# A fused attention and gated-MLP block on one Trainium2 core: the head (loads, modulation, first block of q, k and v) is rebuilt

## The chip, the core and the metric

The kernel runs on one NeuronCore of a Trainium2 chip. The core has five engines with instruction streams of their own: TensorE (PE in the profile; its weight loads are shown apart as PEld), VectorE (DVE), ScalarE (ACT), GpSimd (POOL) and SyncE (SP, which only issues DMAs). They share an on-chip memory of 128 partitions. Matmul results go to PSUM, which has 8 banks of 512 float32 per partition. Engines wait for one another, and for DMAs, by semaphores, and each works strictly in the order of its own stream. The metric is the device time of one execution in microseconds (us); lower is better.

## The reference

x is [2048, 448] in bf16. A conditioning vector c gives six rows of 448 numbers, `silu(c) @ w_mod`: shift, scale and gate for each of two blocks.

```python
mod = (_silu(c) @ w_mod).reshape(c.shape[0], 6, 1, -1)
sa, ca, ga, sb, cb, gb = ...
h = _layernorm(x, axis=-1) * (1 + ca) + sa
x = x + ga * _A_ref(h, A_wqkv, A_wo)
h = _layernorm(x, axis=-1) * (1 + cb) + sb
x = x + gb * _B_ref(h, B_w_in, B_w_sp, B_b_sp, B_w_out)
```

`_A_ref` is attention with 16 heads of 28 dims, causal with a window of 256 keys. `_B_ref` is a gated MLP: `z = gelu(h @ w_in)` with 1792 columns, the second half layer-normed and mixed over the 2048 rows by a 2048 x 2048 matrix, the product of the halves times `w_out`.

## The kernel before, in words

The 2048 rows are 16 tiles of 128 rows (t or j), in four blocks of 512 (tb). The 448 columns of x are four chunks of 128, 128, 128 and 64 (kc or ch).

**The head.** x tiles 0 to 3 (`t_x0`, L415), the first two sixths of w_mod (`t_wmA`, L419: shift and scale of block A) and the q and k columns of wqkv (`t_wq`, L420) are loaded from the SP and ACT queues by `load3` (L406), which puts chunks 0 and 1 into one DMA on ACT and chunks 2 and 3 on SP. The loads of wv, x tiles 4 to 7 and the rest of w_mod (`t_wmB`) wait until `t_wmA` has landed (L422 to L428). c is turned into a column by four small matmuls (L507) and goes through silu. `mod_cols` (L520) multiplies w_mod by it: shift and scale come out as columns (`modT`), one matmul per chunk pair. This is done for block A once w_mod's first part is there (`t_mA`) and for block B later (`t_mB`). The two gates ga and gb are needed along the free axis in all partitions, so the silu column is repeated 128 times (`sc_rep`) and multiplied by w_mod (L574), and VectorE copies the result out (`gg_sb`, L577). GpSimd multiplies wo and w_out by the gates (L580, L929). `warm` (L556) puts matmuls on the identity into gaps of TensorE.

**Block 0** is normed by `stats` (L588: VectorE statistics, GpSimd's reciprocal root) and `norm` (L601), turned on TensorE (L660), scaled and shifted on the way out of PSUM into `hT` (L672/L674, 512 columns), and multiplied by `WQK` (the q and k weights copied to heads of 32, L583) into eight groups of 512 columns (L689) and by wv into V (L742). Block 1 goes the same way. Blocks 2 and 3 are turned by DMA (`turn`, L463) and scaled in place (L653/L655). The q of a block is spread into a block-diagonal buffer `QBD` by four DMAs (L720), whose zeros ACT writes (L516).

**Attention.** For each tile j and each half of the heads: scores (L818 for j 0 and 1, L844 and L853 after), exp on ACT (L805), masks on VectorE (L860, L880), the product with V (L887), the division (L901, L903), a DMA transpose, the product with wo (L912), a second layer norm and another DMA transpose. Then the MLP: the halves of `h @ w_in` (L997, L1018), the mixing matmuls (L1041), add on VectorE (L1045), product on GpSimd (L1048), the product with w_out (L1058), the last add (L1068) and the store (L1073).

**What sets the order.** Every operation is added to a list and gets a number. `ORDER` (L19) is a table that names each operation that is emitted, in order, with its engine (p, a, v, g, s) and the PSUM banks or buffers that it takes. Where an operation may run on two or three engines (`either`, `free`), the table chooses. `Sched.waits` (L208) puts the semaphore waits in. Warm-ups that are not in the table are not emitted. The durations in the code only weigh choices; nothing on the chip waits for them.

Of the kernel before, what the change touches and what calls it, by code (L numbers as in the profile page):

```python
# [4 lines left out]
ACT = mybir.ActivationFunctionType  # L5
# [14 lines left out]
2.a 21.v 30.g 1.s 22.v 23.v 24.v 33.g 34.g 0.a 4.s 31.g 3.a 28.g 25.v 5.s 32.g 6.a 26.v 35.g 50.v 51.p.0 7.s 40.a 8.s 52.p.1 36.g 107.v 53.p.2 109.v  # L20
37.g 108.v 115.v 41.p.0 29.g 38.g 110.v 54.p.3 117.v 39.g 42.a 111.g 43.a 116.v 112.g 118.v 44.a 55.p.4 119.g 113.v.0 45.a 56.p.5 120.g 114.v.1
123.p.1 9.s 121.v.2 49.p.0 122.v.3 10.s 105.a 11.s 106.a 127.p.2 12.s 103.v 104.g 124.p 88.v 128.p 89.v 90.v 13.s 91.v 57.p.3 125.a 129.v 58.p.4 130.a
126.v 131.p.5 59.p.0 132.p 133.p 134.p 136.p.3 135.a 138.p.4 46.a 48.v 146.p.1 147.a 164.v 162.v 168.v 163.v 166.v 167.v 165.v 169.v 170.g 171.g 139.a
142.p.0 143.a 150.s 172.g 151.s 149.s 176.g 174.g 178.g 173.g.0 179.g.1 140.p.2 141.a 137.a 148.s 14.s 16.s 15.s 18.s 17.s 154.p.1 152.p.0 323.p.0
155.v 144.p.1 153.v 145.v 95.p.0 324.a.0 177.v.2 96.v 325.v 175.v.3 327.v 156.p.1 329.p.0 157.a 330.a.1 47.a 97.p.0 98.v 180.p.1 326.p.0 348.p.0 328.p
183.p.0 377.p.0 181.v 182.v 92.p.1 349.a.2 350.a 355.p.0 356.a.3 357.a 331.v 184.v 333.v 185.v 214.v 351.v 94.v 93.v 218.v 158.p.0 332.p 192.p.1 334.p
159.v 186.p.0 375.p.0 193.a 187.a 376.a.4.0 219.v 216.v 27.v 217.v 220.v 215.v 221.v 190.p.1 188.p.0 358.v 335.v 353.v 336.v.0 272.v 191.v 274.v 360.v
273.v 379.v 380.v 270.v 352.p.0 354.p 222.g 223.g 224.g 226.g 228.g 225.g.0 227.g.1 230.g 231.g.2 229.g.3 189.a 378.a 337.s 383.p.0 359.p 160.p.0
385.p.0 198.p.1 361.p 384.a.5.1 161.a 386.a 404.p.0 199.v 362.v 363.v.1 200.p.0 204.p.1 381.p.0 406.p.0 405.a.6.2 407.a 268.v 201.v 409.v 205.v 271.v
388.v 269.v 275.v 387.v 408.v 232.s 235.s 234.s 233.s 196.s 194.s 195.s 197.s 412.p.0 382.p 212.p.0 414.p.0 202.p.1 213.v 413.a.0.3 203.a 433.p.0  # L30
389.p 390.p 210.p.1 208.p.0 434.a.1.4 415.a 209.a 441.p.0 442.a.2.0 417.v 391.v 392.v.2 416.v 410.p.0 411.p 418.p 419.p 437.v 211.v 238.v 435.p.0
# [233 lines left out]
def bass_adaLN_cond__sliding_block__mixer_gmlp__prompt_kernel(  # L265
# [15 lines left out]
    NT = S // 128  # L281
# [859 lines left out]
```

## Time and profile before

| | us |
|---|---|
| median of 3 runs | 281.21 (279.92 to 281.25) |
| profiled execution, first to last instruction (its span; the page gives no other time for it) | 281.0 |
| PE busy | 269.3 |
| DVE busy | 164.3 |
| ACT busy | 128.5 |
| POOL busy | 126.1 |
| start of the first q/k matmul | 15.34 |
| start of the first exp | 23.61 |

The page gives the busy time of each engine, the span in 40 slices, the DMA queues, the chain of work that ended last, and the costliest groups of instructions. A timeline row reads: start, duration, engine, line, operation, tile written <- tile read, count; in brackets the idle time before it and what ended that. A row of the stretches reads: from:to, length, then busy us (and instructions) of PE, PEld, DVE, ACT and POOL, the granted TensorE clock, the share of the DMA engines, and GB/s.

### The profile page before, as it was taken

How to read it: one execution, taken by the hardware profiler on the slowest of the kernel's cores; microseconds unless marked ns; L12 is line 12 of the kernel's file. 1: busy time of each engine (PE TensorE's matmuls, PEld its weight loads, DVE VectorE, ACT ScalarE, POOL GpSimd, SP SyncE). 2: the span in 40 equal slices, each digit the busy share in tenths (PEclk: the TensorE clock that was granted, in tenths of full speed). 3: DMA queues.
4: the chain of work that ended last, by engine and by line, in shares of the span. 5: the costliest groups of instructions: out<-in, count | busy, mean ns of one | idle time of the engine just before them, and what ended most of it. 6: DMA issues, size and time to landing. Idle time of an engine off the chain costs nothing.

```text
span 281.0 us, 7380 instructions
## 1 busy us (share of the span) xinstructions
PE 269.3 (96%) x3198; PEld 142.3 (51%) x3222; DVE 164.3 (58%) x355; ACT 128.5 (46%) x151; POOL 126.1 (45%) x200
## 2 busy tenths in 40 slices
PE   6799999799999999999999999999999999999995
PEld 2445556456657777544444444444444444444452
DVE  6347999599899999968898600000243003124443
ACT  4548899789999999866666700000000000000000
POOL 8231177921027989947769503001477101436110
PEclk9789999999999999999999999999999999999999
DMA  6775735343315485693699989910000000000032
GB/s 199 188 261 157 267 58 98 84 55 72 72 23 75 63 96 80 162 103 79 125 181 186 168 181 201 163 36 0 0 2 0 0 0 2 16 16 16 19 98 98
DMA packets 65347, 26.01 MB, mean 93 GB/s; under 512 B 56418, under 2 KB 64227, under 8 KB 65315
## 3 DMA queue, kind: packets, MB, share of 16 engines
q1 hardware_dynamic: 64496, 24.39, 43.6%
q10 hardware_dynamic: 818, 1.15, 1.5%
q8 instruction: 25, 0.41, 0.6%
q14 instruction: 8, 0.06, 0.1%
HBM read 9.01 MB, written 1.84 MB: 39 GB/s over the span
## 4 chain that ended last, share of the span: by engine, by line
PE 80%; POOL 5%; DVE 4%; ACT 4%; issue 3%; DMA 3%; ACTq 0%; POOLq 0%
PE ps L1041 34%; PE ps L997 8%; PE ps L1058 8%; PE ps L1018 8%; PE ps L689 6%; PE ps L887 4%; ACT PW L805 3%; PE ps L912 3%; DMA wmod<-in_w_mod_dram 3%; PE ps L844 2%; PE ps L742 2%; PE ps L853 1%; POOL xn L610 1%; PE ps L729 1%; POOL wo_g L580 1%
## 5 line engine op out<-in xcount | busy, mean ns | idle before, releaser
L805 ACT ACTIVATE PW<-ps 128x2048 bf16<-128x2048 f32 (+1 forms) x56 | 67.8, 1240 | 4.3 <-PE ps L844 2.6
L1048 POOL TENSOR_TENSOR z1T<-tmpg,z1T 128x512 bf16<-128x512 bf16 x28 | 31.7, 1152 | 77.9 <-DVE tmpg L1045 77.9
L1045 DVE TENSOR_TENSOR tmpg<-ps,bsp_bc 128x512 bf16<-128x512 f32 x28 | 19.0, 689 | 79.2 <-PE ps L1041 70.3
L1041 PE MATMUL ps<-wspB,z 128*128 128x512 bf16 x219 | 49.2, 379 | 0.3
L1041 PE MATMUL ps<-wspA,z 128*128 128x512 bf16 x219 | 48.9, 379 | 0.4 <-issue 0.2
L860 DVE TENSOR_TENSOR PT<-PW,mask 128x1024 bf16<-128x1024 bf16 x56 | 39.2, 729 | 0.3 <-ACT PW L805 0.2
L1041 PEld LDWEIGHTS ps<-wspA,z 128*128 128x128 bf16 x224 | 21.8, 98 | 26.6 <-issue 0.4
L1041 PEld LDWEIGHTS ps<-wspB,z 128*128 128x128 bf16 x224 | 21.9, 98 | 26.3
L596 POOL TENSOR_SCALAR ve_all<-mv_all 128x1 f32<-128x1 f32 (+2 forms) x37 | 11.3, 312 | 46.7 <-DVE mv_all L594 45.9
L689 PE MATMUL ps<-hT,WQK 128*128 128x512 bf16 x98 | 25.5, 388 | 2.4 <-POOL hT L655 1.4
L597 POOL TENSOR_TENSOR rs_all<-ve_all,neghalf 128x1 f32<-128x1 f32 (+2 forms) x37 | 25.3, 694 | 1.1
L887 PE MATMUL ps<-Vaug,PT 128*128 128x32 bf16 x496 | 24.4, 177 | 0.5 <-DVE PT L860 0.5
L887 PEld LDWEIGHTS ps<-Vaug,PT 128*128 128x128 bf16 x496 | 21.8, 96 | 4.4 <-DVE o_sb L903 0.9
L997 PE MATMUL ps<-w_in,hT 64*128 64x448 bf16 x224 | 22.7, 349 | 0.2 <-ACT PW L805 0.2
L1018 PE MATMUL ps<-hT,w_in 64*128 64x512 bf16 x196 | 22.3, 376 | 0.0
L1058 PE MATMUL ps<-w_out_g,z1T 128*128 128x448 bf16 x112 | 21.8, 353 | 0.0
L887 PE MATMUL ps<-Vaug,PW 128*128 128x32 bf16 x224 | 20.2, 176 | 0.0
L591 DVE BATCH_NORM_STATS2 st_all<-x_sb 128x6 f32<-128x448 bf16 x32 | 19.2, 610 | 0.4 <-DMA x_sb<-in_A_x_dram 0.4
L610 POOL TENSOR_SCALAR xn<-x_sb,rs_all,ve_all 128x448 bf16<-128x448 bf16 x22 | 18.9, 863 | 0.3
L887 PEld LDWEIGHTS ps<-Vaug,PW 128*128 128x128 bf16 x224 | 17.6, 96 | 1.9
L591 DVE BATCH_NORM_STATS2 st_all<-z 128x6 f32<-128x448 bf16 x32 | 18.1, 602 | 0.2 <-ACT z L1004 0.2
L1004 ACT ACTIVATE z<-ps 128x896 bf16<-128x896 f32 x16 | 14.1, 915 | 8.3 <-PE ps L997 8.2
(100 smaller groups left out, 333.1 us busy)
## 6 DMA issues: line engine op xcount, KB each, us to landing
out_dram<-fin SPq DMA_DIRECT2D x16, 112.0 KB, 1.7
x_sb<-in_A_x_dram SPq DMA_DIRECT2D x3, 448.0 KB, 4.9
wmod<-in_w_mod_dram SPq DMA_DIRECT2D x1, 1344.0 KB, 8.6
w_in<-in_B_w_in_dram SPq DMA_DIRECT2D x1, 1344.0 KB, 8.9
QBD<-qT SPq DMA_DIRECT2D x16, 64.0 KB, 2.0
w_out_g<-in_B_w_out_dram SPq DMA_DIRECT2D x1, 784.0 KB, 5.3
bsp_bc<-in_B_b_sp_dram SPq DMA_DIRECT2D x1, 512.0 KB, 6.8
wmod<-in_w_mod_dram SPq DMA_DIRECT2D x2, 224.0 KB, 6.1
```

The source lines that it names most:

```text
L591: st = [dve(0.62 if True else 0, lambda e, t=t, ci=ci, s=s: e.bn_stats(st_all[:, slot, t, ci, :], s()), deps(t), prio) for ci, s in enumer ...
L597: rs = pool(0.53 + 0.15 * len(tiles), lambda e: e.tensor_tensor(rs_all[:, slot, a:b], ve_all[:, slot, a:b], neghalf[:, 0:b - a], ALU.pow), ...
L610: "pool": (0.9, lambda e: e.tensor_scalar(to[:, h.slot[0], 0:D], x_sb[:, t, :], z, ve, ALU.mult, ALU.add))}, [nm], prio, [h])
L689: mms = [lambda e, h=h, g=g, kc=kc, tb=tb: e.matmul(ps[:, h.slot[0], :], lhsT=WQK[:, kc, 4 * g:4 * g + 4, :].rearrange("p a b -> p (a b)") ...
L805: ex = act(xdur, lambda e, out_ap=out_ap, in_ap=in_ap: e.activation(out_ap(), in_ap(), ACT.Exp, scale=SCALE), [s], v - 8.0 + u, takes, tab ...
L860: return dve(0.70, lambda e: e.tensor_tensor(cols(hp.slot[0] * 2048 + 1024 * k, [[256, 4], [128, 2], [1, 128]]), cols(at_w() + 128 + 192 * ...
L887: fns.append(lambda e, hp=hp, hO=hO, hi=hi, bi=bi, kb=kb, hd=hd, nb=nb, a=at[hi][bi], p_of=p_of: e.matmul(ps[:, hO.slot[0], 32 * hd:32 * h ...
L997: return lambda e, kc, p0, start, stop: e.matmul(ps[:, hs[t % 2].slot[hf], 0:D], lhsT=hT[p0:p0 + 64, kc, t * 128:(t + 1) * 128], rhs=w_in[ ...
L1018: return lambda e, kc, p0, start, stop: e.matmul(ps[:, hs[b // 2].slot[b % 2], :], lhsT=w_in[p0:p0 + 64, kc, ft * 128:(ft + 1) * 128], rhs ...
L1041: m = pe(16 * MMS, [lambda e, h=h, si=si, ft=ft, tb=tb: e.matmul(ps[:, h.slot[0], :], lhsT=z2[:, si, ft * 128:(ft + 1) * 128], rhs=(wspA i ...
L1048: u = pool(1.16, lambda e, ht=ht, ft=ft, tb=tb: e.tensor_tensor(z1T[tb][:, ft, :], tmpg[:, ht.slot[0], :], z1T[tb][:, ft, :], ALU.mult), [ ...
L1058: return [lambda e, ft=ft: e.matmul(ps[:, h.slot[0], 0:D], lhsT=z1T[t // 4][:, ft, (t % 4) * 128:(t % 4 + 1) * 128], rhs=w_out_g[:, ft, :] ...
```

## The change

- **Loads.** w_mod (first 960 columns now) and the q/k weights come as four row chunks each, alternating between the SP and ACT queues, each with a semaphore of its own. wv, x tiles 4 to 7 and the rest of w_mod no longer wait for `t_wmA`. x tiles 8 to 15 are now issued ahead of the q spread of block 0; in the old order they were issued behind it. wo and w_in still come behind it, with w_in behind block 2's four DMA transposes.
- **Modulation of block A.** A row of ones is put into chunk 3 of w_mod and a 1 into the silu column, so that the matmul also adds the 1 of 1 + scale. The products of each chunk go to columns of their own (8 matmuls per chunk, as each chunk lands), and one VectorE reduction adds them.
- **Gates, and shift and scale of block B.** 16 matmuls in column strips of 32 (`t_rows`) give the four rows; one copy takes them out, two DMAs write them to a DRAM buffer `modrow`, and three DMAs read them back: each gate spread over 128 partitions, shift and scale as columns, four bytes at a time.
- **Block 0** is worked off in two halves of 256 columns. In the first half every q/k group is four matmuls of their own that the order table may mix. Attention of tiles 0 and 1 depends on the first half only.
- **Other.** Three of the four QBD zero fills go from ACT to GpSimd, the first of them ahead of the identity. Warm-ups are one matmul each and use bank 5; 11 are in the table (9 pairs before). The output of tile 1 is made in two halves of 224 columns.
- **The order table** is new from end to end. In it tile 15 is the last output; before it was tile 1. Two of the four scale-and-shift steps of block 2, which ran on GpSimd, are on VectorE and ACT, as are the other two.

```diff
-    t_wmA = load3("d_wmA", wmod, w_mod, slice(0, 2 * D), -98.95, 7.75, 4.5, 6.7)
-    t_wq = load3("d_wq", wq_st, A_wqkv, slice(0, 2 * D), -98.9, 9.6, 8.4, 9.4)
-
-    t_wv = load2("d_wv", "sp", 0.35, wv, ALL, A_wqkv, slice(2 * D, 3 * D), [t_wmA], -95.5)
+    t_wmA = [chunk("d_wmA", ("sp", "act", "sp", "act")[kc], wmod, w_mod, kc, slice(0, 2 * D + 64), -98.95 + 0.001 * kc, LAND_M[kc], 0.23) for kc in range(DC)]
+    t_wq = [chunk("d_wq", ("sp", "act", "sp", "act")[kc], wq_st, A_wqkv, kc, slice(0, 2 * D), -98.9 + 0.001 * kc, LAND_Q[kc], 0.23) for kc in range(DC)]
+
+    t_wv = load2("d_wv", "sp", 0.35, wv, ALL, A_wqkv, slice(2 * D, 3 * D), (), -95.5)
...
-    t_x.append(load_x(1, [t_wmA], -95.0))
-    t_wmB = load2("d_wmB", "sp", 1.4, wmod, slice(2 * D, 6 * D), w_mod, slice(2 * D, 6 * D), [t_wmA], -94.0)
+    t_x.append(load_x(1, (), -95.0))
...
+    t_wmB = load2("d_wmB", "sp", 1.4, wmod, slice(2 * D + 64, 6 * D), w_mod, slice(2 * D + 64, 6 * D), (), -94.0)
...
+    t_qz = [[add({"act": (1.05, lambda e, b=b, q=q: e.activation(QBD[:, b, q].rearrange("p h t -> p (h t)").bitcast(F32), zero[:, 0:1].broadcast_to([128, 1024]), ACT.Copy)),
+                  "pool": (1.3, lambda e, b=b, q=q: e.memset(QBD[:, b, q].rearrange("p h t -> p (h t)").bitcast(F32), 0.0))},
...
+        t_mA.append(pe(0.37, [lambda e, v=v, ch=ch, kc=kc, n=n: e.matmul(
+            ps[:, hA.slot[0], 8 * kc + n:8 * kc + n + 1], lhsT=wmod[:, kc, v * D + ch * 128:v * D + ch * 128 + 128], rhs=sc_sb[:, kc:kc + 1],
+            start=True, stop=True)
...
+    t_modA = [dve(0.16, lambda e: e.tensor_reduce(modT[:, 0:8], ps[:, hA.slot[0], 0:32].rearrange("p (k n) -> p n k", k=4), mybir.AxisListType.X, ALU.add), [t_mA], -59.0)]
...
+    t_rows = pe(0.8, [lambda e, v=v, i=i, kc=kc: e.matmul(
+        ps[32 * i:32 * i + 32, hR.slot[0], 0:D], lhsT=sc_rep[:, kc, :], rhs=wmod[:, kc, v * D:(v + 1) * D],
+        start=(kc == 0), stop=(kc == DC - 1), tile_position=(0, 32 * i)) for kc in range(DC) for i, v in enumerate((2, 5, 3, 4))],
+        [t_wmA, t_wmB, t_screp, t_p2], -15.0, [hR], "cols32")
...
+    t_rowd = [load("d_mr0", "sp", 0.01, lambda e: e.dma_start(modrow[:, 0:D], rows4[0:128:32, :]), [t_rowc], -14.95),
+              load("d_mr1", "sp", 0.01, lambda e: e.dma_start(modrow[2:4, D:DP], rows4[64:128:32, D - 64:D]), [t_rowc], -14.9)]
+    t_gg = [load("d_mg%d" % gi, "sp", 0.1, lambda e, gi=gi: e.dma_start(gg_sb[:, gi, :], modrow[gi:gi + 1, 0:D].broadcast_to([128, D])), [t_rowd[0]], -14.8) for gi in range(2)]
+    t_mc = load("d_mc", "sp", 0.05, lambda e: e.dma_start(modT[:, 8:16], modrow[2:4, :].rearrange("v (c p) -> p (v c)", p=128), allow_slow_non_contiguous=True), [t_rowd], -14.7)
...
+    for half in range(2):
...
+        for g in (0, 4, 1, 5, 2, 6, 3, 7):
+            h = Hold(bA)
+            parts = [lambda e, h=h, g=g, kc=kc, c0=c0: e.matmul(
+                ps[:, h.slot[0], 0:256], lhsT=WQK[:, kc, 4 * g:4 * g + 4, :].rearrange("p a b -> p (a b)"), rhs=hT[:, kc, c0:c0 + 256],
+                start=(kc == 0), stop=(kc == DC - 1)) for kc in range(DC)]
+            m = None
+            if half == 0:
+                for kc in range(DC):
+                    m = pe(0.109, parts[kc], [evs[kc], t_wqk[kc], m], v + 1 + kc * 0.1 + 0.01 * g, [] if kc else [h])
+            else:
+                m = pe(0.436, parts, [evs, t_wqk], v + 1 + 0.1 * g, [h])
...
+            if t == SPLIT:
+                for c0 in (0, 224):
```

The start of each engine's new order, from the table. SP: x tiles 0 and 1; w_mod chunks 0 and 2; q/k chunks 0 and 2; wv; x 4 to 7; rest of w_mod; x 8 to 11; x 12 to 15; write of the rows; two of four q spreads; gate ga; two q spreads; wo; block 2's transposes; w_in. ACT: x 2 and 3; c; w_mod chunks 1 and 3; table load and silu; q/k chunk 1; silu of c; one zero fill; q/k chunk 3; the copies of q/k chunks 1 and 3 with the first scale-and-shift between them. PE: six warm-ups, c, two warm-ups, w_mod chunks 0 to 2, a warm-up, the turn of tile 0, chunk 3, the turn of tile 1, two warm-ups, the turns of tiles 2 and 3, then q and k of the first half. VectorE before those: the copy of q/k chunk 0, the norm of tile 2, the reduction, the norm of tile 3, three scale-and-shifts.

More of the change, by code (lines that the diff above doesn't have):

```diff
@@ L557, in warm @@
+    hA.until += t_modA
+    def warm(n, dur, times, cols):
         for _ in range(n):
[L558 removed]
+            hW = Hold(bH)
             hW.until.append(pe(dur, [lambda e, hW=hW: e.matmul(
[L560 to L565 removed]
```

380 lines of the change are left out of this document (207 added, 173 removed).

## The prediction

> **What bounds the kernel now.** I read the stretches first (busy time of each engine from:to), then the page's DMA issues, then the timeline of each engine over the head.
>
> ```profile
> span 281.0 us, 7380 instructions
> 0.00:15.34 15.34, 10.83 (x70) 5.53 (x72) 7.64 (x26) 7.17 (x10) 7.93 (x21) 0.82 0.73 210
> 15.34:16.60 1.26, 1.26 (x4) 0.45 (x3) 1.04 (x3) 0.00 (x0) 0.00 (x0) 0.50 1.01 393
> 16.60:22.30 5.70, 5.70 (x28) 2.69 (x27) 2.20 (x8) 4.20 (x7) 3.51 (x8) 0.98 0.41 147
> 22.30:60.00 37.70, 34.83 (x705) 20.30 (x712) 33.18 (x72) 33.05 (x35) 19.78 (x27) 1.00 0.52 126
> 60.00:140.00 80.00, 79.16 (x1657) 49.45 (x1661) 73.94 (x160) 68.57 (x75) 47.68 (x85) 1.00 0.53 87
> 160.00:278.00 118.00, 117.37 (x552) 54.67 (x560) 27.60 (x43) 2.06 (x4) 31.72 (x28) 1.00 0.25 50
> 278.00:281.00 3.00, 0.11 (x1) 0.00 (x0) 0.62 (x1) 0.00 (x0) 0.00 (x0) 1.00 0.35 115
> ```
>
> The first busy number is TensorE. From 15.34 to 278 it idles 2.87 us in the stretch from 22.3 to 60 and 0.84 + 0.63 in the two long ones. So the kernel is TensorE's work from the first q/k matmul on, with 15.34 us ahead of it and 3.0 us behind. Two things can shorten it: an earlier start, and less work on TensorE. VectorE and ACT are at 92% and 86% between 60 and 140, so a gain can be lost there, but they are not the bound. The work sum is made against the span of 281.0, 0.2 below the median of the runs (281.21).
>
> What fills the first 15.34 us, from the timeline of TensorE, then the DMA issues (KB each, us from issue to landing) and their issue times:
>
> ```profile
> 9.69 1.47 PE L528 MATMUL ps<-sc_sb,wmod 128*128 128x1 bf16 x32 [1.78 <-DMA wmod<-in_w_mod_dram]
> 11.10 1.46 PE L660 MATMUL ps<-ident,xn 128*128 128x128 bf16 x12
> 12.35 1.92 PE L559 MATMUL ps<-ident 128*128 128x512 bf16 x4
> 15.34 5.84 PE L689 MATMUL ps<-hT,WQK 128*128 128x512 bf16 x23
> wmod<-in_w_mod_dram ACTq DMA_DIRECT2D x1, 448.0 KB, 7.7
> wq_st<-in_A_wqkv_dram ACTq DMA_DIRECT2D x1, 448.0 KB, 8.7
> wq_st<-in_A_wqkv_dram SPq DMA_DIRECT2D x1, 224.0 KB, 7.0
> x_sb<-in_A_x_dram ACTq DMA_DIRECT2D x1, 224.0 KB, 3.2
> x_sb<-in_A_x_dram SPq DMA_DIRECT2D x1, 224.0 KB, 2.9
> 0.79 0.46 SPq L415 DMA_DIRECT2D x_sb<-in_A_x_dram  x1
> 1.94 0.40 ACTq L409 DMA_DIRECT2D wmod<-in_w_mod_dram  x1
> 2.37 0.49 ACTq L409 DMA_DIRECT2D wq_st<-in_A_wqkv_dram  x1
> 2.43 0.57 SPq L410 DMA_DIRECT2D wq_st<-in_A_wqkv_dram  x1
> ```
>
> TensorE waits for w_mod until 9.69, then does the 32 modulation products, the turns, and warm-ups up to 15.34. The granted clock is 0.50 from 15.34 to 16.60 (second row of the stretches): the first 1.26 us of real work ran at half rate.
>
> **Landing times.** The ACT part of w_mod lands at 1.94 + 7.7 = 9.64 and q/k chunk 2 (SP) at 9.43. By then ACT's queue has delivered x, and w_mod, 672 KB (224 + 448), SP's 784 KB (x 224, w_mod 224 + 112, q/k 224): 1456 KB at 9.5. All 2016 KB are there at 2.37 + 8.7 = 11.07. The first 448 KB (x) land at 0.79 + 2.9 to 3.2, say 3.8. I interpolate between these three points, with both queues served alike. After the change, w_mod is complete when SP has delivered 224 + 240 + 240 = 704 KB and ACT 584 to 704, 1288 to 1408 KB: 8.6 to 9.2, say 8.9. Q/k chunk 0 (SP 928 KB, ACT 808 to 928) comes at 10.3 to 10.6, say 10.45; the last q/k chunk at about 11.2, as before. Bytes set this, not the number of pieces; loads that no longer wait lie behind in SP's queue, though ACT's last q/k chunk, issued only after the silu and a zero fill (about 7.3), shares with them.
>
> **The head, step by step.** Durations are from these rows of VectorE, GpSimd, ACT and TensorE:
>
> ```profile
> 11.12 0.40 DVE L584 COPY WQK<-wq_st 128x896 bf16<-128x896 bf16 x1 [2.65 <-DMA wq_st<-in_A_wqkv_dram]
> 6.75 0.70 DVE L604 TENSOR_SCALAR xn<-x_sb,mv_all,rs_all 128x448 bf16<-128x448 bf16 x2 [0.46 <-POOL rs_all L597]
> 12.60 1.00 DVE L674 TENSOR_SCALAR hT<-ps,modT 128x512 bf16<-128x512 bf16 x2 [0.83 <-PE ps L660]
> 5.72 2.00 ACT L516 ACTIVATE QBD<-zero 128x1024 f32<-128x1024 f32 x2
> 10.95 0.95 ACT L583 ACTIVATE WQK<-wq_st 128x896 bf16<-128x896 bf16 x1 [0.50 <-DMA wq_st<-in_A_wqkv_dram]
> ```
>
> TensorE: w_mod at 8.9, two modulation groups (1.47 / 4 = 0.37 each), a warm-up (1.92 / 4 = 0.48), a tile's four turns (1.46 / 3 = 0.49): all products done at 10.6. VectorE has meanwhile stood before the copy of q/k chunk 0, behind which the norm of tile 2 and the reduction are queued: 10.45 + 0.40, norm 0.35, reduction about 0.15 (as the four small ones it replaces, an estimate), norm of tile 3 0.35, first scale-and-shift 0.25 to 0.5 (half of, or all of, a 512-column one): 12.0. TensorE has the turns of tiles 2 and 3 before its first q/k matmul, the latter ready at 11.7 + 0.49 = 12.2. First q/k matmul at 12.3, with bounds 11.6 (w_mod and q/k chunk 0 0.7 sooner) and 13.3 (w_mod no sooner than 9.64). **Gain 3.0.** Chunk 3 of q/k lands at 11.2, its copy takes ACT 0.95, and its first user comes after 13 matmuls and V of tile 0: that slack is about 3 us.
>
> **The clock takes half of it back.** Before, dense 512-column matmuls ran from 12.35 and full rate came at 16.60, 4.25 later. After, turns and single-column products fill 9 to 12.3, with three warm-ups between; they also filled 9.69 to 12.35 before, without release. Counting 4.25 from 12.3 gives full rate at 16.5. Then 4.2 us pass at half rate, a loss of 2.1 against 0.63 before: **cost 1.5**, with bounds 0 (release at 13.5) and 3.2 (release at 20). The Trainium skill ("TensorE: Matmul & The Clock Gate", Part 1) says the gate looks at a free-running window of about 3.4 us, releases after a busy one, and the phase varies between runs; by it the release is estimated between 3.4 and 6.8 us after dense work begins. The 4.25 agrees, and the rule's late end is the rival below.
>
> **Work taken off TensorE,** and put on:
>
> ```profile
> 23.83 0.92 PE L574 MATMUL ps<-wmod,sc_rep 128*128 128x448 bf16 x4
> 25.87 0.93 PE L574 MATMUL ps<-wmod,sc_rep 128*128 128x448 bf16 x4
> 26.63 0.61 PE L660 MATMUL ps<-ident,xn 128*128 128x128 bf16 x8
> 28.55 0.57 PE L528 MATMUL ps<-sc_sb,wmod 128*128 128x1 bf16 x13
> 29.67 0.17 PE L533 MATMUL ps<-sc_sb,wmod 128*64 128x1 bf16 x1
> L997 PE MATMUL ps<-w_in,hT 64*128 64x448 bf16 x224 | 22.7, 349 | 0.2 <-ACT PW L805 0.2
> ```
>
> The gates cost 0.92 + 0.93; the last 0.17 of a group overlaps the next one (the second starts at 25.87, the turns behind it at 26.63, 0.76 later), so they take 1.5 to 1.8, say 1.7. Block B's modulation runs from 28.55 to 29.84: 1.3. Together 3.0 go. The 16 strip matmuls of 448 columns cost 16 x 0.19 = 3.0 if they run one after another, 0.8 if four strips run at once (0.19 = 0.76 / 4, one of L574's). No strip of 448 columns is in this trace; the nearest row is L997, where two half-height tiles run together: 22.7 / 224 = 0.10 each, half of 0.19. I take 1.0. **Gain 2.0** (bounds 0 and 2.2). The Trainium skill ("TensorE: Matmul & The Clock Gate", Part 3) gives 2.38 times for three strips at once; as an estimate, 3.0 / 2.4 = 1.3 and a gain of 1.7, which changes little.
>
> **What costs nothing, and under what cover.** The gate path through DRAM: row copy, a write (a store lands in 1.7 us here), a read; gates are first used by wo's products on GpSimd, which ran from 44.79 on before.
>
> ```profile
> 44.79 1.45 POOL L580 TENSOR_TENSOR wo_g<-wo_g,gg_sb 128x448 bf16<-128x448 bf16 x1
> out_dram<-fin SPq DMA_DIRECT2D x16, 112.0 KB, 1.7
> w_in<-in_B_w_in_dram SPq DMA_DIRECT2D x1, 1344.0 KB, 8.9
> QBD<-qT SPq DMA_DIRECT2D x16, 64.0 KB, 2.0
> 29.00:30.00 1.00, 0.84 (x29) 0.72 (x28) 1.00 (x4) 0.97 (x2) 0.00 (x0) 1.00 1.05 405
> 52.54 0.81 PE L689 MATMUL ps<-hT,WQK 128*128 128x512 bf16 x3 [1.44 <-POOL hT L655]
> 22.32 1.28 ACT L805 ACT_TABLE_LOAD   x1
> 23.61 1.02 ACT L805 ACTIVATE PT<-ps 128x1024 bf16<-128x1024 f32 x1
> ```
>
> So there are 20 us of cover; what it holds up is SP, where gate ga's read waits for the write to land, with two q spreads, wo and block 2's turns behind it: about 2 us, against QBD's first use two attention tiles later. Zero fills leave ACT for GpSimd: 3 x 1 us off ACT; GpSimd's first one delays the identity by some 1.0 (ACT's time for it, an estimate), thus the warm-ups, under the wait for w_mod. VectorE loses two gate copies. 32 more q/k matmuls with weight loads hide under streaming (PEld 20.30 of 37.70): 0 to +0.4, I take 0.2. Eight more evictions lie on ACT, idle 1.5 of 5.7 from 16.6 to 22.3. First exp: half 0's 32 matmuls (14 at half rate to 16.5, 18 x 0.11), one more group and the scores, then the 1.28 us table load, at about 21 instead of 23.61. The output of tile 1 in halves is not last in the table; 0. The 1.44 us idle at 52.54 is a wait for GpSimd, which the change relieves (scale-and-shift of block 2 goes to VectorE and ACT), while w_in now sits behind block 2's turns and before block 1's q spread on SP. Bounds -1.4 and +3; I take +0.5 for waits that a wholly new order brings.
>
> **Sum:** -3.0 + 1.5 - 2.0 + 0.2 + 0.5 = -2.8; 281.2 - 2.8 = 278.4.
>
> **Rivals.**
> - *The gate opens late, or the loads are no sooner.* Full rate at 20 instead of 16.5 costs 1.75; w_mod at 9.64 costs 0.7 to 1.0. Either alone gives 279.4 to 280.2, both 281. For: the loads before were bound by bytes, and the bytes are the same. Against: q/k work no longer waits for block 0 as a whole.
> - *SP's queue makes it slower.* w_in took 8.9 us to land among other loads. Issued after block 2's turns, it stands before block 1's q spread and tile 0's output turn, behind the gate read that itself waits. If the spread lands as late as w_in did (8.9 against a usual 2.0), the scores of tiles 4 to 7 wait, ACT runs dry and TensorE, in order, idles up to 6.9 us: 278.4 + 6.9 = 285.3, partly covered 283. It decides once waits between 22 and 60 grow from 2.87 by 2.8 + 1.4, to over 7. For: the stretch is the only one with idle TensorE now. Against: at the 405 GB/s of the row from 29 to 30 w_in is 3.4 us, and the spread is issued some us after it.
> - *Better than forecast.* The idle at 52 goes (-1.4, and my +0.5), the clock opens at 15: 275.8.
>
> **How the numbers follow.** The forecast's own case, 277.0 to 279.8, has 0.37; better 0.20; the late gate or loads, 279.8 to 282.6, 0.19; SP's queue, or another wait of the new order, slower than that, 0.24. A measurement of this kernel can tell about 0.5% (1.4 us) from no change. Faster: 0.37 + 0.20 and a few hundredths of the third case, 0.59; same 0.17; slower 0.24. Range 275.6 to 283.2: it leaves out a tenth on each side; the likeliest case's own range is 277.0 to 279.8.
>
> **What the profile after would show.** First q/k matmul at 12.3 and full clock at 16.5; modulation products in four groups as chunks land; 16 strip matmuls within 1.0 us near 21; first exp near 21; no gate work on VectorE; TensorE idle between 22 and 60 at or under 3. I am wrong if the first q/k matmul starts after 14, if the clock stays at half past 18, or if the idle between 22 and 60 is above 7 with QBD or the turns as releaser.

## The result

The changed kernel takes 295.33 us (median of 4 runs, 294.42 to 296.32) against 281.23 for the kernel before: 1.0501 times as long, with a 95% interval of 1.044 to 1.0561. The forecast was 278.4 with a range of 275.6 to 283.2. It was wrong in sign and by 17 us. Three single runs further down, of body_only (301.91), order_to_113 (291.71) and tail_only (301.31), took over 1.5% more than the fastest run of the same kernel and are left out of the medians.

### The profile after, read as before

The stretches of the changed kernel (from:to, length, then busy us and instructions of PE, PEld, DVE, ACT and POOL, the granted TensorE clock, DMA share, GB/s):

```profile
span 293.7 us, 7405 instructions
0.00:13.51 13.51, 7.81 (x63) 3.89 (x64) 11.40 (x24) 4.95 (x8) 9.77 (x22) 0.88 0.90 274
13.51:16.90 3.39, 3.39 (x15) 1.97 (x14) 1.84 (x6) 0.62 (x2) 0.00 (x0) 0.50 1.05 310
22.30:60.00 37.70, 34.77 (x707) 20.52 (x699) 35.50 (x77) 32.04 (x35) 18.21 (x28) 1.00 0.48 111
60.00:108.00 48.00, 46.05 (x1166) 30.83 (x1162) 44.51 (x98) 43.34 (x44) 21.31 (x40) 1.00 0.37 65
108.00:122.00 14.00, 10.89 (x201) 6.07 (x200) 9.65 (x19) 9.64 (x12) 3.88 (x6) 0.76 0.76 126
122.00:140.00 18.00, 17.60 (x206) 8.73 (x202) 13.79 (x35) 11.50 (x16) 11.80 (x27) 1.00 0.68 121
140.00:172.51 32.51, 27.27 (x264) 12.52 (x261) 20.46 (x56) 21.21 (x35) 13.62 (x36) 1.00 1.01 167
172.51:290.70 118.19, 118.09 (x567) 55.31 (x567) 28.16 (x44) 0.00 (x0) 35.62 (x32) 1.00 0.16 35
```

The head gains, if less than forecast: the first q/k matmul starts at 13.51 instead of 15.34 (forecast 12.3), and full clock comes at 16.9 (forecast 16.5). The stretch from 22.3 to 60 idles 2.93 us, as much as before (2.87). The loss lies behind it. 172.51 is where the mixing matmuls (L1084) start. Between 22.3 and there TensorE idles 2.93 + 1.95 + 3.11 + 0.40 + 5.24 = 13.6 us. In the kernel before, the mixing started at 160.28, and these rows give the idle time up to it:

```profile
22.30:60.00 37.70, 34.83 (x705) 20.30 (x712) 33.18 (x72) 33.05 (x35) 19.78 (x27) 1.00 0.52 126
60.00:108.00 48.00, 47.52 (x1235) 32.88 (x1238) 46.57 (x97) 45.56 (x47) 23.57 (x39) 1.00 0.43 70
108.00:122.00 14.00, 13.64 (x252) 7.97 (x252) 11.92 (x27) 12.16 (x14) 12.10 (x23) 1.00 0.83 124
122.00:140.00 18.00, 18.00 (x176) 8.61 (x174) 15.45 (x38) 10.86 (x16) 12.01 (x24) 1.00 0.53 102
140.00:160.28 20.28, 20.12 (x194) 9.30 (x192) 18.08 (x47) 13.59 (x24) 15.47 (x33) 1.00 1.07 181
```

2.87 + 0.48 + 0.36 + 0 + 0.16 = 3.9 us. So 9.8 us (13.63 less 3.87) of the 12.7 us between the spans (293.7 and 281.0) are new waits of TensorE. Another part is the clock: three stretches around 113 us show it at half.

```profile
108.00:112.90 4.90, 2.59 (x88) 1.74 (x85) 3.40 (x7) 4.30 (x5) 2.38 (x4) 0.98 1.18 111
112.90:113.70 0.80, 0.00 (x0) 0.00 (x1) 0.00 (x0) 0.00 (x0) 0.00 (x0) 0.50 0.59 123
113.70:119.50 5.80, 5.80 (x89) 3.09 (x90) 4.09 (x7) 2.85 (x4) 1.49 (x2) 0.50 0.75 193
```

5.8 us of work at half rate cost 2.9 us. The two make 12.7 us, but the q/k work also starts 1.8 us sooner, so this account leaves some 2 us of loss unnamed. About 1.1 of them are the half clock of the head (1.7 us lost between 13.51 and 16.90, against 0.63 before).

The waits have names. TensorE's waits of the changed kernel (us in total, times, longest), and the four long ones in the timeline, with the idle time ahead of the row and what ended it in brackets:

```profile
PE ps L954 <- DMA hT<-o_sb: 4.5, 3, 2.9
PE ps L1084 <- DMA wspA<-in_B_w_sp_dram: 3.8, 1, 3.8
PE ps L742 <- DVE Vaug L789: 2.8, 2, 2.2
PE ps L1039 <- POOL hT L979: 1.5, 1, 1.5
48.88 1.04 PE L742 MATMUL ps<-hT,WQK 128*128 128x512 bf16 x4 [2.24 <-DVE Vaug L789]
113.70 1.68 PE L954 MATMUL ps<-wo_g,hT 128*128 128x448 bf16 x4 [2.87 <-DMA hT<-o_sb]
149.01 1.31 PE L1039 MATMUL ps<-w_in,hT 64*128 64x448 bf16 x12 [1.46 <-POOL hT L979]
172.51 13.99 PE L1084 MATMUL ps<-wspA,z 128*128 128x512 bf16 x64 [3.79 <-DMA wspA<-in_B_w_sp_dram]
```

Four different producers: a copy on VectorE, an output turned by DMA, a scale-and-shift on GpSimd, a weight turned by DMA. None is in the rebuilt head. The page's chain that ended last says the same in one line, first of the kernel before, then of the changed one:

```profile
PE 80%; POOL 5%; DVE 4%; ACT 4%; issue 3%; DMA 3%; ACTq 0%; POOLq 0%
```

```profile
PE 53%; DVE 15%; SPq 14%; DMA 10%; ACT 3%; POOL 2%; issue 2%; DVEq 0%
```

SP issues every DMA transpose, one after another, some 1.3 us each. SP's timeline, before and after, shows the last turned h of the second norm (hT<-xn) and the last run of wspA ahead of the mixing:

```profile
134.23 1.26 SPq L467 DMA_TRANSPOSE hT<-xn  x1
135.54 19.94 SPq L467 DMA_TRANSPOSE wspA<-in_B_w_sp_dram  x14
```

```profile
107.52 0.58 SPq L563 DMA_DIRECT2D gg_sb<-modrow  x1
108.16 1.20 SPq L478 DMA_TRANSPOSE hT<-o_sb  x1
142.95 2.57 SPq L478 DMA_TRANSPOSE hT<-xn  x2
162.30 7.29 SPq L478 DMA_TRANSPOSE wspA<-in_B_w_sp_dram  x4
```

Before, the turned h were out at 135.5 and wspA at 155.5. After, they are out at 145.5 and 169.6. The order table puts wspB transposes between the wspA ones, and a read of the gate gb through DRAM (107.52) stands ahead of the turn (108.16) that TensorE waits for at 113.70.

### The profile page after: what moved, and what is told of

Read it like the earlier page. It is cut to its first block, busy times and chain, and to the rows that moved or that the text cites. A ratio compares the mean times of both kernels' runs of the same rounds, so it can differ in the third digit from the quotient of the medians.

```text
span 293.7 us, 7405 instructions
## 1 busy us (share of the span) xinstructions
PE 271.4 (92%) x3222; PEld 143.6 (49%) x3222; DVE 170.7 (58%) x367; ACT 127.5 (43%) x155; POOL 115.9 (39%) x192
## 4 chain that ended last, share of the span: by engine, by line
PE 53%; DVE 15%; SPq 14%; DMA 10%; ACT 3%; POOL 2%; issue 2%; DVEq 0%
PE ps L1084 28%; SPq L478 13%; PE ps L1101 7%; DMA hT<-o_sb 4%; DVE st_all L577 4%; PE ps L929 3%; PE ps L954 3%; DVE PT L902 2%; PE ps L886 2%; DVE xn L590 2%; PE ps L784 2%; ACT PW L847 2%; PE ps L742 2%; DMA hT<-xn 2%; PE ps L895 2%
## 5 line engine op out<-in xcount | busy, mean ns | idle before, releaser
L1084 PE MATMUL ps<-wspA,z 128*128 128x512 bf16 x224 | 49.5, 379 | 3.8 <-DMA wspA<-in_B_w_sp_dram 3.8
L1084 PE MATMUL ps<-wspB,z 128*128 128x512 bf16 x224 | 50.0, 379 | 0.1
L902 DVE TENSOR_TENSOR PT<-PW,mask 128x1024 bf16<-128x1024 bf16 x56 | 38.6, 716 | 1.3 <-ACT PW L847 1.3
L1084 PEld LDWEIGHTS ps<-wspA,z 128*128 128x128 bf16 x224 | 21.8, 98 | 30.5 <-DMA wspA<-in_B_w_sp_dram 4.3
L1084 PEld LDWEIGHTS ps<-wspB,z 128*128 128x128 bf16 x224 | 21.9, 98 | 26.6 <-DMA wspB<-in_B_w_sp_dram 0.6
L583 POOL TENSOR_TENSOR rs_all<-ve_all,neghalf 128x1 f32<-128x1 f32 (+2 forms) x37 | 23.6, 653 | 1.3
L1039 PE MATMUL ps<-w_in,hT 64*128 64x448 bf16 x224 | 22.4, 349 | 1.6 <-POOL hT L979 1.5
L742 PE MATMUL ps<-hT,WQK 128*128 128x512 bf16 x80 | 20.3, 380 | 2.8 <-DVE Vaug L789 2.8
L1101 PE MATMUL ps<-w_out_g,z1T 128*128 128x448 bf16 x105 | 20.7, 352 | 0.0
L954 PE MATMUL ps<-wo_g,hT 128*128 128x448 bf16 x64 | 16.1, 381 | 4.5 <-DMA hT<-o_sb 4.5
## 6 DMA issues: line engine op xcount, KB each, us to landing
x_sb<-in_A_x_dram SPq DMA_DIRECT2D x3, 448.0 KB, 12.3
```

The source lines that it names most:

```text
L583: rs = pool(0.53 + 0.15 * len(tiles), lambda e: e.tensor_tensor(rs_all[:, slot, a:b], ve_all[:, slot, a:b], neghalf[:, 0:b - a], ALU.pow), ...
L742: m = pe(4 * MMS, [lambda e, h=h, g=g, kc=kc, tb=tb: e.matmul(ps[:, h.slot[0], :], lhsT=WQK[:, kc, 4 * g:4 * g + 4, :].rearrange("p a b -> ...
L902: return dve(0.70, lambda e: e.tensor_tensor(cols(hp.slot[0] * 2048 + 1024 * k, [[256, 4], [128, 2], [1, 128]]), cols(at_w() + 128 + 192 * ...
L954: mo = pe(4 * MMD, [lambda e, h=h, j=j, ch=ch: e.matmul(ps[:, h.slot[0], 0:D], lhsT=hT[:, ch, j * 128:(j + 1) * 128], rhs=wo_g[:, ch, :], ...
L1039: return lambda e, kc, p0, start, stop: e.matmul(ps[:, hs[t % 2].slot[hf], 0:D], lhsT=hT[p0:p0 + 64, kc, t * 128:(t + 1) * 128], rhs=w_in[ ...
L1084: m = pe(16 * MMS, [lambda e, h=h, si=si, ft=ft, tb=tb: e.matmul(ps[:, h.slot[0], :], lhsT=z2[:, si, ft * 128:(ft + 1) * 128], rhs=(wspA i ...
```

## The experiments

The theory (A): the rewritten order of the body, behind the head, makes the loss, and the rebuilt head gains about what its trace shows. The rivals: the head itself leaves something behind (B), the path through DRAM clogs SP (C), the interleaved wspB does it (D), or one early stretch does it and the rest follows (G). In the grafts further down, theory A is put as F, that waits at many places add up, and rival H is that SP, once late, does not catch up. An entry of the order table reads number.engine.slot. In a graft of one table on another, the few bank and buffer slots that clash at the seam were renamed, and some entries there come a little later.

### Head and body apart

`head_only`: the new head, then the old order. The table is the changed kernel's for 222 entries, with the late DMAs of the path through DRAM moved into them.

```diff
-    SPLIT = 1
+    SPLIT = -1
...
 ... 317.v 275.g 278.g.0 18.s 196.v 202.a
-422.p.0 319.v 274.g.1 237.p.0 248.v 423.a.4.0
+422.p.0 20.s 19.s 372.v 373.p.0 375.p 424.p.0
```

> The changed kernel's head (its code, and its order table up to the second half's last q/k copy and V2's), and behind it the order that the kernel before has, with the engines and buffers that it names; mr1, gg1 and mc are issued in the head, the output tile 1 is left whole. Theory A (the loss is in the rewritten order of the body, the rebuilt head gains what its trace shows, 2.1 us at the first exp and 3.3 us at j2's scores): about 278, between 276.5 and 280.5. Rival B (the rebuilt head costs it: what its queues and its gates through DRAM leave behind): 290 or more. In between, 281 to 289: the new head does not fit the old body, and some of the loss is theirs together.

`body_only`: the kernel before, whose table goes on in the changed kernel's order behind V3's copy.

```diff
 ... 383.p.0 359.p 160.p.0 385.p.0 198.p.1 361.p 384.a.5.1 161.a 386.a
-404.p.0 199.v 362.v 363.v.1 200.p.0
+204.p.0 205.v 233.s 232.s 404.p.0 271.v
```

> The kernel before with its own head up to V3's copy, and behind it the changed kernel's order of the same operations. Theory A: the rewritten body alone costs about 295.3 minus 278 = 17 us, so about 297 (293 to 300). Rival B: within 2 us of before, 279 to 283.

Measured: body_only 297.4 us, 1.0583 times before (1.0493 to 1.0674); head_only 285.38, 1.0167 times (1.0098 to 1.0236). The new order on the old head costs 16.6 us by itself (297.4 against 280.8 beside it), so theory A holds for the loss and B falls. How much of the 16.6 is made at the seam itself was not measured. Its trace has the two largest waits of the changed kernel (4.5 and 3.8 us) at much the same size, on the lines of the old code:

```profile
PE ps L912 <- DMA hT<-o_sb: 4.3, 3, 1.8
PE ps L1041 <- DMA wspA<-in_B_w_sp_dram: 3.5, 1, 3.5
```

With the new head the same order is 2.1 us faster (297.4 against 295.3), so the head is worth about that much there, though the intervals of the two overlap. But head_only shows no gain. Its timeline has TensorE waiting 3.1 us between 30 and 40, where the seam had put three q products of block 1 into one bank, and block 0's q spread behind a gate read. `head_seam` mends that:

```diff
-... 206.s ... 207.s ... 102.s ... 208.s ... 205.s 103.s 104.s
+... 206.s ... 207.s ... 208.s ... 205.s 102.s
-... 375.p 424.p.0 ... 235.p.0
+... 375.p ... 235.p.0 424.p.0
-... 404.a 247.p.1 374.v
+... 243.p.0 247.p.1 428.p.0 ... 252.s 103.s 104.s
```

> As head_only, with its seam mended: the gate read gg0 behind block 0's q spread, gg1 and mc behind block 1's, block 1's k3 product where the kernel before has it (in head_only it held a bank, so that q0, q1 and q2 of block 1 took turns in one bank), and j2's QBD product behind q1 and q2. Theory A (the head alone gains what body_only against the changed kernel shows, 3.2 us at the first Wo product, and head_only lost 3.1 us of it to TensorE's waits between 30 and 40): TensorE waits under 1 us between 30 and 40, time 278 (276.5 to 280). Rival: the q spread of block 0, issued 5 us later than before, holds j2 and then everything: 282 to 285.

Measured: 281.49, 1.004 times before (1.0014 to 1.0066). The waits at the seam are gone, mostly, and still the head gains nothing on the old body: 278 was wrong, and so is the half of theory A that gave the head 3 us anywhere. Two timeline rows show where the lead goes, head_seam's here and the one of before that the prediction quotes (52.54, 1.44 idle, released by GpSimd's hT):

```profile
50.84 0.81 PE L742 MATMUL ps<-hT,WQK 128*128 128x512 bf16 x3 [1.21 <-POOL hT L714]
```

Both kernels wait there for block 2's scale-and-shift on GpSimd, and head_seam gets it only 1.7 us sooner. At the mixing it leads by 1.5 (158.82 against 160.28). That is against one profiled execution of before, which took longer than the median (below); against the median nothing is left.

### Single waits and SP's queue

All five start from the changed kernel. `v7_first` moves V7's copy:

```diff
-... 410.v.1 481.a.1.4 ... 489.a.2.0 260.v 249.s
+... 410.v.1 260.v 481.a.1.4 ... 489.a.2.0 249.s
```

> The changed kernel with one instruction moved: V7's copy on DVE ahead of the four masks, behind j1's o. If TensorE's waits add up, the 2.24 us at 48.9 go and the time is 293.1 (292.5 to 293.7). Rival: what follows waits for the same transposes and masks anyway, and the time stays at 294.5 to 296.

Measured: 293.32 (292.11 to 294.78), 2.0 us under the changed kernel. The wait at 48.9 is gone and the time falls by nearly all of it. This one wait, at least, was paid in full, as far as medians of four runs can tell.

`dram_early` moves the late DMAs of the path through DRAM:

```diff
-... 100.s ... 205.s ... 485.v 101.s ... 580.v 104.s ... 618.v 103.s
+... 100.s 101.s ... 205.s 103.s 104.s ... 485.v ... 580.v ... 618.v
```

> The changed kernel with three DMAs of the path through DRAM moved up on SP: mr1 right behind mr0, gg1 and mc right behind the last q spread of block 0; nothing else moves. Theory C (the late gate read gg1 at 107.5 us is what holds the transposes behind it, costs 2.87 us at L954 and then 3.3 us of a halved clock, and mc costs some at 68): about 289 (287.5 to 291). Theory A says that these are small against the order: 293 to 296.

Measured: 294.50 (294.21 to 295.36), only 0.8 less, within the spread of the runs. L954's waits for hT<-o_sb fall from 4.5 to 4.0 us in all, the longest from 2.9 to 1.7. In its trace the clock stays at 1.00 from 113 to 122 and falls behind the wait for wspA instead (0.56 from 170.14 to 174). Theory C falls: the gate read makes the wait longer, it does not make it.

`wo_later` moves two Wo products (and the two additions behind them) back on TensorE:

```diff
-... 642.v.2 615.p.1 534.g ... 685.p.0 616.v ... 712.p.0 696.v
+... 642.v.2 534.g ... 685.p.0 ... 712.p.0 615.p.1 616.v 696.v
-... 757.v 702.p.0 758.v.0 ... 807.p.0 703.v ... 777.p 704.v
+... 757.v 758.v.0 ... 807.p.0 ... 777.p 702.p.1 703.v 704.v
```

> The changed kernel with two Wo products moved back on TensorE: j8's behind j12's first scores, j11's behind j14's third PV product, so that their transposed o has landed (4.5 and 5.5 us after its issue). If the waits add up: 1.3 and 2.9 us go, and with the second the fall of the clock behind it (3.3 us): 287.8 to 291.2. Rival: the transposes are late because SP is late, and the next product that needs one waits in its place: 294 to 296.

Measured: 296.19 (294.25 to 298.65), no gain. One row shows why: the next Wo product waits just as long.

```profile
115.54 1.67 PE L954 MATMUL ps<-wo_g,hT 128*128 128x448 bf16 x4 [3.00 <-DMA hT<-o_sb]
```

`wspa_first` puts all wspA transposes ahead of the wspB ones in the same places; `wspa_up` moves five wspA transposes to right behind w_out's load:

```diff
-... 877.s ... 856.s ... 872.s ... 881.s ... 857.s ... 867.s
+... 856.s ... 857.s ... 867.s ... 858.s ... 861.s ... 865.s
...
```

```diff
-... 369.s 801.p.0 ... 861.s ... 855.s ... 853.s ... 854.s ... 852.s
+... 369.s 861.s 855.s 852.s 853.s 854.s 801.p.0 ...
```

> The changed kernel with all 16 wspA transposes ahead of the 16 wspB in the same places of SP's list. Theory D (the wspB ones issued between make L1084 wait 3.8 us for wspA): that wait goes, 291 to 292. Rival: the loss is made before, and TensorE then waits elsewhere (for wspB at the end of the stage): 294.5 to 296.

> The changed kernel with five wspA transposes (9, 3, 0, 1, 2) moved up on SP to right behind w_out's load, where SP waits from 115.5 to 120.8 us. The last wspA then lands some 6.5 us sooner: L1084's wait of 3.8 us goes, 291.5 (291 to 292.5). Rival: as with wspa_first, the wait comes back as one for wspB or for the late hT: 294.5 to 297.

Measured: wspa_first 296.87 (296.46 to 297.50), somewhat above its rival's range, and wspa_up 294.42 (293.75 to 295.55). TensorE's waits, of wspa_first and then of wspa_up, the latter with a row of SP's timeline:

```profile
PE ps L1084 <- DMA wspB<-in_B_w_sp_dram: 4.6, 1, 4.6
```

```profile
PE ps L954 <- DMA hT<-o_sb: 8.8, 3, 3.4
112.36 1.68 PE L954 MATMUL ps<-wo_g,hT 128*128 128x448 bf16 x4 [2.97 <-DMA hT<-o_sb]
130.27 0.93 PE L954 MATMUL ps<-wo_g,hT 128*128 128x448 bf16 x4 [2.50 <-DMA hT<-o_sb]
134.57 1.67 PE L954 MATMUL ps<-wo_g,hT 128*128 128x448 bf16 x4 [3.37 <-DMA hT<-o_sb]
114.94 12.32 SPq L478 DMA_TRANSPOSE wspA<-in_B_w_sp_dram  x6
```

In each the wait that was aimed at goes, and another takes its place: with wspA first, wspB is late; with wspA early, the turned outputs queue behind it (SP spends 12.32 us on six wspA in a row, and the next turned output is issued at 127.30 instead of 122.04). So D falls too. Behind 100 us the waits share one queue, SP's, which this order fills late; the scale-and-shift on GpSimd, too, waits for turned h (3.0 us in the changed kernel). In these two runs moving an item in that queue moved the wait.

### How much each stretch of the order costs

Three grafts keep the changed kernel's order up to some point and go on in the old one; a fourth followed while the last stretch was open. What of gg1 and mc stands behind a cut is issued in the head. The table is cut at 330, 560, 700 and 800 entries. The first cut:

```diff
 ... 290.v 108.g 436.p 462.a 300.v 437.p
-331.g 509.p.0 438.v 325.g 332.g.0 439.v.2
+255.p.0 256.a 438.v 439.v.2 463.v 457.p.0
```

> The changed kernel's order up to where its trace stands at some 45 us (330 entries of its table), and behind it the order of the kernel before for all that is left; output tile 1 whole, gg1 and mc issued in the head. Theory F (the loss is the sum of waits spread over the new order, each at its place): none of the waits of the changed kernel from 46 us on is there, so about the time of head_seam, 281.5 (280.5 to 283.5). Rival G (one early stretch of the order does it, all later waits follow from it): 288 or more.

> The same with 560 entries, up to some 87 us. Theory F: the 2.24 us at 48.9 and the 0.5 at 76 are in it, the rest is not: 284.2 (283 to 286). Rival G: near 281.5 or above 289.

> The same with 700 entries, up to some 113 us. Theory F: the waits of 1.3 us at 90 and 2.9 at 113 come to it, and the fall of the clock behind the second where it happens (3.3 us): 288.4 without, 291.7 with it (287 to 292). The waits for hT at 149 and for wspA at 172 (5.3 us together) stay out unless SP is by then so late that it can't catch up (rival H: then 293 or more).

> The changed kernel's order up to 800 entries, some 131 us, and behind it the order of the kernel before. If the last 7.3 us are the waits for hT and wspA behind 140 us (1.5 and 3.8) with what the clock adds: 288 to 290.5. If they are made between 113 and 131, where the clock is at half for 6.6 us: 291.5 or more.

| new order up to | us (median) | times before (95%) | added |
|---|---|---|---|
| the head only (head_seam) | 281.5 | 1.0014 to 1.0066 | |
| 45 us (order_to_45) | 283.0 | 1.0037 to 1.0095 | 1.5 |
| 87 us (order_to_87) | 286.4 | 1.0108 to 1.0239 | 3.4 |
| 113 us (order_to_113) | 287.1 | 1.0137 to 1.0273 | 0.7 |
| 131 us (order_to_131) | 291.1 | 1.0339 to 1.0398 | 4.0 |
| the end (changed kernel) | 295.3 | 1.044 to 1.0561 | 4.2 |

The loss grows along the order, as theory F has it. G falls, and H too: with the old order behind 113 us the rest runs without a wait for wspA.

The sizes of the steps, however, do not fit the waits that F named for them. V7's copy is entry 319, so its wait of 2.24 us, which I had expected behind the first cut, is in the 1.5 of that step; the step up to 87 us adds 3.4 all the same, and 286.4 is above the 283 to 286 expected. For the step up to 113 us F named two waits for turned outputs, 4.2 us without the clock, and 0.7 came: order_to_113's trace has no wait of L954 for hT<-o_sb. The grafts also have waits of their own behind the seam (L895 and L1039 for ACT: 1.4 and 1.4 us in order_to_87, 1.3 and 2.0 in order_to_113). So a step is not the price of its stretch, and none is surer than the intervals (about 2 us). order_to_131 lies above its first expectation: of the 8 us behind 113, about half arise up to 131.

`tail_only` is the reverse, head_seam up to 113 us and then the changed kernel's order:

```diff
 ... 754.v 748.p 800.a.2.2 565.v
-364.v 852.s 838.g 772.p.0 773.a 755.p
+755.p 651.v.2 756.p 838.g 780.p.0 566.s
```

> head_seam up to where the changed kernel's table stands at some 113 us, and behind it the changed kernel's order of what is left. If the last stretch of the new order costs by itself what it adds in the whole (295.3 minus 288.0 = 7.3 us): 281.5 + 7.3 = 288.8 (287 to 291), with TensorE waiting for hT from GpSimd near 145 and for wspA near 165. If that stretch costs only because SP comes into it late from the earlier ones: 281 to 284.

Measured: 299.1 (296.15 to 300.32), 1.0595 times before. It is above its expectation because the seam waits too: TensorE is busy only 15.23 of the 21 us from 92 to 113, where several products of the old order had to come late. The two waits asked about are there:

```profile
PE ps L1084 <- DMA wspA<-in_B_w_sp_dram: 3.5, 1, 3.5
PE ps L1039 <- POOL hT L979: 2.0, 1, 2.0
```

So the last stretch waits even if what stands ahead of it is the old order, with the seam's own waits between the two. Its price apart from the seam stays open.

### The head's first surprise, mended

In the changed kernel the second norm of block 0 takes 2.62 us and the next two 1.10 and 1.00, where the first takes 0.40. VectorE's and GpSimd's timelines of the changed kernel:

```profile
7.22 0.40 DVE L590 TENSOR_SCALAR xn<-x_sb,mv_all,rs_all 128x448 bf16<-128x448 bf16 x1 [0.39 <-POOL rs_all L583]
8.00 2.62 DVE L590 TENSOR_SCALAR xn<-x_sb,mv_all,rs_all 128x448 bf16<-128x448 bf16 x1
10.94 1.10 DVE L590 TENSOR_SCALAR xn<-x_sb,mv_all,rs_all 128x448 bf16<-128x448 bf16 x1
8.16 1.22 POOL L506 MEMSET Vaug<- 128x256 bf16 x1
8.96 1.53 POOL L505 MEMSET Vaug<- 128x768 bf16 x1
10.72 2.20 POOL L530 MEMSET QBD<- 128x1024 f32 x2
```

The long norm ends 0.13 us after the second memset; the two of some 1 us lie beside QBD's memsets, the short one where there is none. `head_quiet` is head_seam with GpSimd's memsets out of the way:

```diff
-... 51.a 117.g ... 10.a 55.p ... 122.p 40.g ... 123.v 39.g ... 183.v 42.g ... 181.a 49.g ... 149.p 50.g
+... 51.a 40.g 39.g 42.g 117.g ... 10.a 49.a 50.a 55.p ... 122.p ... 123.v ... 183.v ... 181.a ... 149.p
```

> head_seam with GpSimd silent while DVE normalises block 0: the two Vaug memsets and the mask's go up ahead of the first ve on GpSimd, the two QBD memsets go to ACT behind its last load issue. If GpSimd's memsets are what makes the second norm take 2.62 us and the third and fourth 1.0 to 1.1: each takes about 0.4, the first q/k product comes at 12.2 instead of 13.45, and the time falls by 0.6 to 1.2 us, to about 280.5, level with before or just under it. If not: the norms stay long and the time within 0.4 of head_seam.

```profile
8.37 0.40 DVE L590 TENSOR_SCALAR xn<-x_sb,mv_all,rs_all 128x448 bf16<-128x448 bf16 x1
8.94 0.40 DVE L570 COPY WQK<-wq_st 128x896 bf16<-128x896 bf16 x1 [0.18 <-DMA wq_st<-in_A_wqkv_dram]
9.25 0.39 DVE L590 TENSOR_SCALAR xn<-x_sb,mv_all,rs_all 128x448 bf16<-128x448 bf16 x1
10.61 0.63 PE L645 MATMUL ps<-hT,WQK 128*128 128x256 bf16 x2
18.56 1.02 ACT L847 ACTIVATE PT<-ps 128x1024 bf16<-128x1024 f32 x1
```

Measured: 279.8 us (12 runs, 278.73 to 280.59), 0.9952 times before (0.9926 to 0.9978), the one kernel here that is faster than before, if only by 0.5%. Every norm takes 0.39 to 0.40, the first q/k matmul comes at 10.61 (13.45 in head_seam, 15.34 before), the first exp at 18.56. Of 2.8 us sooner at the q/k matmul, 1.7 remain at the end, more than the 0.6 to 1.2 expected.

`quiet_v7` mends both on the changed kernel: head_quiet's moves and v7_first's.

> The changed kernel with two things mended: GpSimd's memsets moved as in head_quiet, and V7's copy ahead of the masks as in v7_first. If the losses add up: 295.3 minus 2.0 minus 1.7 (head_quiet against head_seam) = 291.6 (290.5 to 292.5). If what a quicker head gains is lost again behind SP's queue: 293 or more.

Measured: 292.69 (291.85 to 293.42). It is 0.6 under v7_first, not 1.7. Its wait for wspA is 0.8 us longer than v7_first's 4.3, which is most of what is missing:

```profile
PE ps L1084 <- DMA wspA<-in_B_w_sp_dram: 5.1, 1, 5.1
```

So the quicker head arrives sooner at SP's late transposes and waits there.

## Why the prediction was wrong

**First q/k matmul at 12.3: measured 13.51,** 0.2 outside its bounds. Not the loads: TensorE had w_mod at 8.59, and head_quiet's copy of q/k chunk 0 was released at 8.94, 1.5 us sooner than my 10.45. What I priced at 0.35, the norm, took 2.62 beside Vaug's memsets. These ran on GpSimd before, too, but ahead of the norms (from 2.28 to 4.62); the new order puts them behind the reciprocal roots, beside the norm. The next two norms, 1.10 and 1.00, lie beside QBD's zero fills, which the change moved from ACT. I counted those as relief for ACT and asked only what they delay on GpSimd. So the gain of the earlier start was 1.8, not 3.0.

**Full clock at 16.5 for 1.5 us: close, in part by luck.** It came at 16.9, and 3.39 / 2 = 1.7 us were lost against the 2.1 of the sum. But the count behind it, 4.25 us, does not hold: from the first q/k matmul to full clock it is 3.39 us here and, estimated from the clock of the stretches, some 2.5 in head_seam and 2.2 in head_quiet. A later start and a shorter count happened to cancel.

**Work off TensorE, gain 2.0: the strips right, the sum not borne out.** The 16 strips took 0.94 us against 1.0 assumed:

```profile
21.59 0.94 PE L554 MATMUL ps<-wmod,sc_rep 128*32 128x448 bf16 x16
21.55 1.02 ACT L847 ACTIVATE PT<-ps 128x1024 bf16<-128x1024 f32 x1
```

The estimate of 1.3, made from a figure of the Trainium skill ("TensorE: Matmul & The Clock Gate", Part 3) for three strips, is above what the trace shows for four. The first exp came at 21.55, forecast 21.

What came off TensorE in sum can be estimated: the time from the first q/k matmul to the mixing, less the idle time and half of the time at half clock. Before takes 144.94 - 3.87 - 0.70 = 140.4 us, head_seam 145.37 - 5.00 - 1.24 = 139.1, the changed kernel 159.00 - 13.63 - 5.21 = 140.2. So of 1.8 us (2.0 less the 0.2 for the extra matmuls) the old order shows 1.2, the new order 0.2. Why the new order loses the rest stays open.

**"+0.5 for waits that a wholly new order brings", bounds -1.4 and +3: this is the step that failed.** It measures +16.6 on the old head (body_only). I read the stretch with idle time, 22 to 60, as the only place where waits could grow, and took the 0.84 us between 60 and 140 for a property of the kernel. It was a property of the old table: every operand arrived just ahead of its use because each entry had been placed so. A new table has to earn that again at some 1,190 entries, and nothing in the profile of before says that it will. My own sign of being wrong, idle time between 22 and 60 above 7, did not show (2.93), while the loss stood behind it. The nearest rows for a bound were not those of 22 to 60. They were SP's: behind the last turned h it issued 14 wspA transposes in 19.94 us, and the mixing used them 4.8 us after the last one (155.48, 160.28). A wspA transpose there lands 3.4 to 5.6 us after its issue (median 4.2), and the last was issued at 154.2, so only some 2 us of this were slack (an estimate). In the changed kernel the turned h come 10 us later; TensorE, held up by the earlier waits, comes to the mixing 8.4 us later (168.72 against 160.28) and still waits 3.8.

**The base of the sum.** I set the span of 281.0 beside the median of 281.2. In the runs of before made beside the experiments the time is 1.7 to 1.8 us over the span, so the profiled execution of before took about 282.7, an estimate from that difference. These runs sort by granted clock: at 1.0 the median is 280.0 (16 runs), at 0.994 281.0 (25 runs), at 0.988 282.6 (one run). The page's execution had 0.988. So part of what the head can gain, the half-clock time before 16.6, is a loss that most executions of before have less of or not at all. This goes with head_seam's being 1.5 us ahead in the trace and level in time: its runs at 0.986 to 0.988 took 281.2 to 282.2 (six runs), and those at 0.999 to 1.0 took 280.7 to 281.3 (three runs), no less than before at 1.0.

**The rivals.** "SP's queue makes it slower" had the right engine and the wrong place and transfers: it priced block 1's q spread between 22 and 60 at up to 6.9 us, and the waits came from transposes behind 80, and one from V7's copy at 48.9. Its chance of 0.24 took in "another wait of the new order", but the prices that stood beside it, 283 to 285.3, were 10 us too small. "The gate opens late, or the loads are no sooner" did not occur. The head's gain itself, forecast at 2.8 to 3.3, is about 2.1 on the new order, none on the old one until GpSimd's memsets are moved (head_quiet, about 1.3).

## What to carry to other kernels

A rewritten order can be the largest part of a change that contains one, whatever else the diff says: price it from the slack of each in-order queue (when the last DMA transpose is issued against when it is used), in the stretches that do not wait now. If it can be split off, put the old order behind the new head first; here that and five moved operations of GpSimd (four memsets and the mask's) make 279.8 us out of 295.3. And when a wait is mended, look at what the same queue delivers next before counting the gain.

## What the runs showed of the hardware

- **GpSimd memsets held up VectorE's bf16 norm.** It took 0.40 us alone, 2.62 beside two Vaug memsets, 1.0 to 1.1 beside QBD's. VectorE's statistics were not touched: in head_quiet they ran beside the same Vaug memsets in 0.62 and 0.59 us. The Trainium skill ("SBUF — State Buffer", Who interferes with whom) says that VectorE in its two-port modes and GpSimd hold one port pair exclusively and that the loser waits for the whole instruction; this trace agrees on the blocking, and the wait here ran through two memsets: the norm ended just behind the second (10.62 and 10.49). It does not show who came first, since the norm's row starts 0.16 us ahead of the memset's and GpSimd's spans are rough.
- **A short wait can cost the clock, a longer one need not.** In the changed kernel a wait of 2.87 us ahead of 113.70 came with 6.6 us at half clock from 112.9 on, some 2 us into the wait; the wait of 3.79 us ahead of 172.51 came with none (1.00 in the next row). Nor did length decide it at the mixing in other runs: a wait of 4.17 us (wo_later) left the clock at 1.00, and behind 3.49 (tail_only) and 3.52 (body_only) it was 0.58 and 0.64 for the next 4 us. The Trainium skill ("TensorE: Matmul & The Clock Gate", HAM oscillation — how this bites in real kernels) gives gaps over about 3.4 us as the danger. By these rows that is no safe limit from either side. What decides it these runs do not show.
- **A DMA transpose landed late with others under way.** The turn issued at 108.16 was used at 113.70, 5.5 us later. A gate read had been issued just ahead of it (107.52, 4.1 us to landing), and three more turns were issued up to 112.03; the median of the three turned outputs issued from 107 to 115 was 3.9 us. Which of these made it late is not shown.
